# One reordered opening, one load queue and block-wise exponentials in a fused sparse-attention and three-way-maximum kernel

## The chip, the cores and the metric

The kernel runs on one core of a Trainium2 chip. The metric is device microseconds (us) of one execution, the median of several; lower is better. The core has a matrix engine (TensorE, PE in the profile, with its weight loads as PEld), a vector engine (VectorE, DVE), an activation engine (ScalarE, ACT), a general engine (GpSimd, POOL), a sequencer that only issues transfers here (SyncE, SP) and 16 DMA engines. Each engine works through its own instructions in order; semaphores tie them together.

## The reference

```python
# q, k, v: (8, 8, 576, 64); heads 0-3 local, heads 4-7 strided
scores = matmul(q, k.T) / sqrt(64)
mask_local   = (rel >= 0) & (rel < 32)                 # rel = row - column
mask_strided = (rel >= 0) & (column % 32 == row % 32)
attn = softmax(where(mask, scores, -1e9))              # max subtracted, sum + 1e-9
x = matmul(attn, v) -> (4608, 512)                     # heads beside one another
h = maximum(maximum(x @ w1, x @ w2), x @ w3)           # w1, w2, w3: (512, 768)
out = h @ w_out                                        # w_out: (768, 512)
```

The four weight matrices arrive as float32 bits that were widened on the host to 64-bit words; the kernel turns each of them into a high and a low part. The same is done with x and h, and every product is taken as three matmuls (high x high, high x low, low x high).

## The kernel before

**Units.** Attention is cut into 32 units, four for each of the 8 batches: two strided pairs of heads, then two local pairs (line 195). Unit n needs its queries and keys (`load_qk`, two transfers of 288 KB) and its values (`load_v`, four or five small transfers). Its steps are S (scores on PE into PSUM), X (on VectorE: the mask from batch 1 on, the row maximum and its subtraction), E (one exponential over the whole unit on ScalarE), N (on VectorE: sums, reciprocal, product, transpose), V (values on PE into the one PSUM tile `o`), H and L (the high part of x on ScalarE, the low part on VectorE).

**Chunks.** The feed-forward part runs over nine chunks of 512 rows. For a chunk, F0 to F17 are the 18 products with the blocks of w1, w2 and w3 (12 matmuls each), M the maxima behind them, O0 to O3 the products with w_out (18 matmuls each) and Q the stores. f0, f1 and g0, g1 are the halves of F0 and F1: f for the strided heads, g for the local ones.

**Weights.** 24 blocks of weights of 512 KB (w0 to w17 for F0 to F17, w18 to w23 for w_out) are converted on the chip, in five steps over four functions: A (line 145: magnitude of the high words, ScalarE; line 146: the low words, ScalarE; line 147: clamp, GpSimd), B (lines 158 and 161: bits put together, VectorE, with a quarter of the PSUM tile `o` as scratch), D (line 171: low bits added, GpSimd), C (line 179: high part, ScalarE; line 180: low part, GpSimd). The magnitude lives in one of three buffers of the pool `wk` from A to the end of C.

**The opening.** Chunk 0 is the opening: units 0 to 7, all 24 conversions, F0 to F17 and O0 to O3 of chunk 0, laid out by the string `OPENING` (lines 47 to 55), which is a fixed order of steps; each engine gets its instructions in that order and keeps it. From chunk 1 on a loop with fixed places does the rest (lines 513 to 552); the change doesn't touch it. Unit 8's scores (S8) are part of the opening, its later steps belong to chunk 1.

**Sharing in the opening.** V writes the four banks of `o`, H and L read them, and B uses columns of the last two of them: the waits in the trace show that V, H and B take turns. The scores of units 0 and 2 lie in a PSUM tile that is given up before f0, those of the others in a second one.

**Loads.** Two queues issue loads at the start (lines 479 to 493): SP takes the queries and keys of units 0 to 3 first, ScalarE's queue takes w0, the values of unit 0, w1 and w2. SP then takes v1, w3, v2, w4, v3, w5 to w8, q4, v4, w9 to w13, q5, v5 and the rest. Loads for units 6 on are issued behind S4, S5, V4 and so on.

Of the kernel before, what the change touches and what calls it, by code (L numbers as in the profile page):

```python
# [7 lines left out]
F32 = mybir.dt.float32  # L8
# [3 lines left out]
AF = mybir.ActivationFunctionType  # L12
ALU = mybir.AluOpType
AX = mybir.AxisListType

B, H, S, D = 8, 8, 576, 64
# [27 lines left out]

OPENING = """
S0 X0 S1 E0 N0 A0 X1 B0 D0 E1 V0 A1 S2 C0 A2 N1 B1 H0 B2 D1 L0 A3 S3 C1 A4 X2 E2 B3 B4 D2 D3 C2 D4 A5 X3
C3 C4 N2 V1 H1 A6 B5 D5 L1 f0 A7 E3 B6 B7 C5 V2 D6 A8 C6 N3 D7 H2 f1 B8 U4 S4 D8 C7 A9 L2 V3 C8 X4 H3 L3
A10 A11 B9 D9 B10 D10 g0 g1 E4 M0 F2 M1 C9 C10 F3 N4 A12 A13 M2 U5 B11 B12 M3 D11 B13 D12 D13 F4 S5 C11  # L50
M4 C12 A14 C13 F5 A15 M5 X5 B14 F6 M6 B15 E5 D14 F7 M7 A16 D15 C14 V4 F8 F9 C15 B16 M8 N5 A17 A18 B17
B18 D16 F10 M9 F11 M10 H4 D17 C16 S6 C17 D18 A19 A20 F12 M11 M12 X6 B19 B20 C18 F13 D19 E6 M13 A21 D20
F14 L4 C19 F15 N6 C20 A22 V5 M14 B21 H5 L5 B22 D21 A23 F16 B23 S7 D22 M15 C21 F17 C22 D23 V6 M16 M17 C23
O0 O1 Q0 X7 E7 H6 L6 Q1 N7 O2 V7 U8 O3 H7 Q2 Q3 L7 S8
"""


@with_exitstack
def fused_kernel(ctx, tc, qT, kT, qk_loc, qk_str, v_loc, v_str, m_loc, m_str, w1, w2, w3, w_out, out):
# [6 lines left out]
    att = ctx.enter_context(tc.tile_pool(name="att", bufs=2))  # L66
    hp = ctx.enter_context(tc.tile_pool(name="hp", bufs=NJ))
    hm = ctx.enter_context(tc.tile_pool(name="hm", bufs=2))
    wk = ctx.enter_context(tc.tile_pool(name="wk", bufs=3))

    xp = [ctx.enter_context(tc.tile_pool(name=f"xp{i}", bufs=1)) for i in range(2)]
    early = ExitStack()
# [65 lines left out]
    def convert_begin():  # L138


        raw, i, j = raws.pop(0)
        words = raw.rearrange("p (n two) -> p n two", two=2)
        low, high = words[:, :, 0], words[:, :, 1]
        mag = wk.tile([P, 512], F32, name="work")
        pin(nc.scalar.activation(out=mag, in_=high.bitcast(F32), func=AF.Abs))
        pin(nc.scalar.activation(out=low, in_=low.bitcast(U32), func=AF.Copy, scale=2.0**-29))
        pin(nc.gpsimd.tensor_scalar(out=mag, in0=mag, scalar1=W_MOST, scalar2=W_LEAST, op0=ALU.min, op1=ALU.max))  # L147
        begun.append((low, high, mag, i, j))

    converted = []  # L150

# [46 lines left out]
    def load_qk(n):  # L198
        if n >= len(units):
            return  # L200
        b, p = units[n]
        t = (io_early if n in (2, 3) else io).tile([P, 2, S], F32, name="qk_t", bufs=2)
        if b < EARLY:
            pin(nc.sync.dma_start(out=t[:, 0, :], in_=qT[b, p]))
            pin(nc.sync.dma_start(out=t[:, 1, :], in_=kT[b, p]))
        else:
            src = qk_loc[b - EARLY, p, 0] if p < 2 else qk_str[b - EARLY, p - 2].rearrange("p x s -> p (x s)")
            src = src.rearrange("p (x h s) -> p x h s", x=2, h=2)
            for h in range(2):
                hs = slice(h * D, (h + 1) * D)  # L210
                pin(nc.sync.dma_start(out=t[hs], in_=src[hs, :, h, :]))
        loaded[n] = [t.rearrange("p x s -> p (x s)")]
# [99 lines left out]
    def less_maximum(n):  # L312
        s_ps, s, wide, nm, at, axes, masked = state[n]
        if masked:
            flat, mask = masked
            pin(nc.vector.tensor_tensor(out=flat, in0=flat, in1=mask.broadcast_to(list(flat.shape)), op=ALU.add))
        mx = att.tile([P, 2, MS], F32, name="mx")
        pin(nc.vector.tensor_reduce(out=mx[:, :, :nm], in_=s, op=ALU.max, axis=axes))  # L318
        pin(nc.vector.tensor_tensor(out=s, in0=s, in1=wide(mx), op=ALU.subtract))  # L319

    def exponentials(n):
        s = state[n][1]
        pin(nc.scalar.activation(out=s, in_=s, func=AF.Exp, scale=SCALE))  # L323

    def probabilities(n):
        s_ps, s, wide, nm, at, axes, _ = state[n]
        sm = att.tile([P, 2, MS], F32, name="sm")

        sums = sm[:, :, :nm] if nm * at == 512 else s_ps[:, :, 512 - MS : 512 - MS + nm]
        pin(nc.vector.tensor_reduce(out=sums, in_=s, op=ALU.add, axis=axes))  # L330
        pin(nc.vector.tensor_scalar(out=sums, in0=sums, scalar1=EPS, scalar2=None, op0=ALU.add))
        pin(nc.vector.reciprocal(out=sm[:, :, :nm], in_=sums))
        pin(nc.vector.tensor_tensor(out=s, in0=s, in1=wide(sm), op=ALU.mult))  # L333
        state[n] = s_ps, nm, at
# [141 lines left out]
        pin(nc.scalar.dma_start(out=out[c * CH + t * P : c * CH + (t + 1) * P, :], in_=o_sb))  # L476


    for n in range(4):
        load_qk(n)  # L480
    pin(nc.scalar.activation(out=nothing, in_=nothing, func=AF.Exp))
    load_weights(1, nc.scalar)
    load_v(0, nc.scalar)
    load_weights(2, nc.scalar)
    load_v(1)
    for n in (2, 3):
        load_weights(1)
        load_v(n)
    for count, n in ((4, 4), (5, 5)):
        load_weights(count)  # L490
        load_qk(n)
        load_v(n)
    load_weights(len(sources))
    steps = {
        "U": paired_queries, "S": scores, "X": less_maximum, "E": exponentials, "N": lambda n: (probabilities(n), transposed(n)),
        "V": values, "H": leading, "L": rest,
        "A": lambda n: convert_begin(), "B": lambda n: convert_bits(), "D": lambda n: convert_add(),
        "C": lambda n: convert_end(),
        "F": lambda n: ff_in(0, n // 3, n % 3), "f": lambda n: ff_in(0, n // 3, n % 3, (2, 3)),
        "g": lambda n: ff_in(0, n // 3, n % 3, (0, 1)), "M": lambda n: ff_max(0, n // 3, n % 3),  # L500
# [118 lines left out]
```

## Time and profile before

| | |
|---|---|
| time, median of 3 runs | 707.14 us (707.0 to 708.51) |
| the profiled execution's own time | 705.32 us |
| its span, first to last instruction | 703.6 us |
| TensorE busy | 677.2 us (96%) |
| VectorE, ScalarE, GpSimd busy | 297.2, 188.8, 151.1 us |
| start of chunk 1 on TensorE (behind S8) | 122.99 us |
| moved by DMA | 55.67 MB |

The page cuts the span into 40 slices of 17.6 us, with one digit for each engine, and gives the granted clock of TensorE in tenths of full speed. Views by window give the busy time of each engine in a stretch; the timeline gives instructions with their start, duration and the idle time ahead of them; the waits sum that idle time by what ended it. GpSimd's last conversion, and TensorE's wait for it, stand near 107 us.

### The profile page before, as it was taken

To read this page: it belongs to the slowest core of one execution; us is meant where nothing else is said; L and a number is where in the kernel's file an instruction comes from. 1 tells how busy PE (TensorE), PEld (TensorE's weight loads), DVE (VectorE), ACT (ScalarE), POOL (GpSimd) and SP (SyncE) were. 2 spreads that over 40 slices of the span, in tenths; PEclk is the share of its full clock that TensorE was granted. 3 is DMA by queue.
4 is the path that set the end of the run, shared out by engine and by line. 5 is a ranking of instruction groups with operands and counts; after the bars stand their busy time and mean duration, and the time that the engine had idled before them with its cause. 6 is when DMAs were issued, how large, how long until landed. Compare 5 with 4: busy or idle time off the path is not lost.

```text
span 703.6 us, 16737 instructions
## 1 busy us (share of the span) xinstructions
PE 677.2 (96%) x7408; PEld 555.2 (79%) x7408; DVE 297.2 (42%) x507; ACT 188.8 (27%) x402; POOL 151.1 (21%) x153
## 2 busy tenths in 40 slices
PE   4579999999999999999999999999999999999997
PEld 3457877888888888878888888888888888888886
DVE  5788782754425540555145434544255101101110
ACT  2576653222122122222221312222212111111111
POOL 5789891011000110111011000110010101100120
PEclk9879999999999999999999999999999999999999
DMA  9998122312212221222211132223120010010001
GB/s 266 255 275 331 56 63 99 105 56 65 94 47 66 94 80 45 61 75 70 96 56 55 65 110 70 57 65 94 52 56 2 22 40 0 1 46 15 1 1 60
DMA packets 36081, 55.67 MB, mean 79 GB/s; under 512 B 5257, under 2 KB 18569, under 8 KB 36009
## 3 DMA queue, kind: packets, MB, share of 16 engines
q1 hardware_dynamic: 29060, 43.30, 21.1%
q10 hardware_dynamic: 6948, 11.31, 4.5%
q8 instruction: 58, 0.95, 0.6%
q14 instruction: 15, 0.11, 0.1%
HBM read 45.15 MB, written 9.44 MB: 78 GB/s over the span
## 4 chain that ended last, share of the span: by engine, by line
PE 84%; POOL 3%; DVE 1%; issue 1%; ACT 0%; DVEq 0%; ACTq 0%
PE f_ps L445 56%; PE f_ps L470 21%; PE o_ps L366 2%; PE o_ps L396 2%; PE s_ps L273 2%; PE s_ps L295 2%; POOL wNone L180 1%; POOL work L171 1%; POOL hl L461 0%; DVE work L161 0%; DVE o_ps L158 0%; POOL w L180 0%; POOL work L147 0%; DVE xl L428 0%; ACT xh L424 0%
## 5 line engine op out<-in xcount | busy, mean ns | idle before, releaser
L445 PE MATMUL f_ps<-xh,w 128*128 128x512 f32 x1296 | 410.2, 393 | 3.2 <-DVE pt L340 2.7
L445 PEld LDWEIGHTS f_ps<-xh,w 128*128 128x128 f32 x1296 | 244.3, 188 | 56.2 <-ACT w L179 2.7
L445 PE MATMUL f_ps<-xl,w 128*128 128x512 f32 x648 | 253.7, 391 | 0.9 <-DMA qk_t<-in_kT 0.5
L457 DVE TENSOR_TENSOR h_max<-f_ps,h_max 128x512 f32<-128x512 f32 x108 | 74.3, 688 | 290.6 <-PE f_ps L445 290.6
L461 POOL TENSOR_TENSOR hl<-h_max,hh 128x512 fp32r<-128x512 f32 x54 | 69.5, 1287 | 518.1 <-ACT hh L460 518.1
L445 PEld LDWEIGHTS f_ps<-xl,w 128*128 128x128 f32 x648 | 122.2, 189 | 26.5 <-DVE xl L428 1.9
L470 PE MATMUL f_ps<-wNone,hh 128*128 128x512 f32 x432 | 134.6, 392 | 0.5 <-POOL wNone L180 0.5
L470 PEld LDWEIGHTS f_ps<-wNone,hh 128*128 128x128 f32 x432 | 80.4, 188 | 17.8 <-POOL wNone L180 0.9
L460 ACT CAST hh<-h_max 128x512 fp32r<-128x512 f32 x54 | 33.4, 618 | 200.8 <-DVE h_max L457 200.8
L470 PE MATMUL f_ps<-wNone,hl 128*128 128x512 f32 x216 | 84.1, 389 | 0.0
L428 DVE TENSOR_TENSOR xl<-o_ps,xh 128x320 fp32r<-128x320 f32 (+11 forms) x96 | 28.3, 350 | 56.5 <-ACT xh L424 45.6
L475 ACT COPY work<-f_ps 128x512 f32<-128x512 f32 x36 | 21.2, 590 | 102.1 <-PE f_ps L470 102.1
L455 ACT COPY h_max<-f_ps 128x512 f32<-128x512 f32 x54 | 31.7, 588 | 60.4 <-POOL hl L461 33.1
L470 PEld LDWEIGHTS f_ps<-wNone,hl 128*128 128x128 f32 x216 | 40.6, 188 | 8.7 <-issue 0.2
L323 ACT ACTIVATE s_ps<-s_ps 128x640 f32<-128x640 f32 (+2 forms) x32 | 20.7, 648 | 91.7 <-DVE s_ps L319 84.1
L340 DVE STREAM_TRANSPOSE pt<-s_ps 128x640 f32<-128x640 f32 (+2 forms) x32 | 32.4, 1012 | 0.7
L424 ACT CAST xh<-o_ps 128x320 fp32r<-128x320 f32 (+11 forms) x96 | 24.3, 328 | 29.5 <-PE o_ps L396 18.8
L318 DVE TENSOR_REDUCE mx<-s_ps 128x10 f32<-128x640 f32 (+2 forms) x32 | 24.7, 772 | 6.7 <-PE s_ps L295 5.7
L333 DVE TENSOR_TENSOR s_ps<-s_ps,sm 128x640 f32<-128x640 f32 (+2 forms) x32 | 25.0, 780 | 1.1
L319 DVE TENSOR_TENSOR s_ps<-s_ps,mx 128x640 f32<-128x640 f32 (+2 forms) x32 | 25.0, 780 | 1.1
L295 PE MATMUL s_ps<-qk_t 64*32 64x64 f32 (+1 forms) x1408 | 19.7, 227 | 5.2 <-issue 3.1
L171 POOL TENSOR_TENSOR work<-work,w 128x512 int32<-128x512 int32 x18 | 23.2, 1299 | 5.2 <-DVE work L161 4.5
(52 smaller groups left out, 355.9 us busy)
## 6 DMA issues: line engine op xcount, KB each, us to landing
out<-work ACTq DMA_DIRECT2D x36, 256.0 KB, 2.1
qk_t<-in_qT SPq DMA_DIRECT2D x28, 288.0 KB, 3.9
qk_t<-in_kT SPq DMA_DIRECT2D x28, 288.0 KB, 4.8
w<-in_w SPq DMA_DIRECT2D x15, 512.0 KB, 8.2
v_t<-in_v_str SPq DMA_DIRECT2D x56, 128.0 KB, 3.3
v_t<-in_v_loc SPq DMA_DIRECT2D x48, 96.0 KB, 3.3
wNone<-in_w_out SPq DMA_DIRECT2D x6, 512.0 KB, 11.5
w<-in_w ACTq DMA_DIRECT2D x3, 512.0 KB
```

The costliest lines, as they stand in the source:

```text
L171: pin(nc.gpsimd.tensor_tensor(out=bits, in0=bits, in1=low, op=ALU.add))
L295: pin(nc.tensor.matmul(s_ps[32 * j : 32 * (j + 1), h, k1 : k1 + w], t[hs, q0 : q0 + 32], t[hs, k0 : k0 + w], start=not first, stop=not fir ...
L319: pin(nc.vector.tensor_tensor(out=s, in0=s, in1=wide(mx), op=ALU.subtract))
L333: pin(nc.vector.tensor_tensor(out=s, in0=s, in1=wide(sm), op=ALU.mult))
L340: pin(nc.vector.transpose(pt[:, :, : nm * at], s_ps[:, :, : nm * at]))
L428: pin(nc.vector.tensor_tensor(out=lo, in0=src, in1=hi.bitcast(F32), op=ALU.subtract))
L445: pin(nc.tensor.matmul(f_ps, w[:, kc, :], x[:, kc, :], start=(kc == 2 and n == 0), stop=(kc == 1 and n == 2)))
L455: pin(nc.scalar.copy(out=a, in_=f_ps))
L457: pin(nc.vector.tensor_tensor(out=a, in0=f_ps, in1=a, op=ALU.max))
L460: pin(nc.scalar.copy(out=hh, in_=a))
L461: pin(nc.gpsimd.tensor_tensor(out=hl, in0=a, in1=hh.bitcast(F32), op=ALU.subtract))
L470: pin(nc.tensor.matmul(f_ps, h[:, ts], w, start=(j == 0 and n == 0), stop=(j == NJ - 1 and n == 2)))
```

## The change

The string of the opening is replaced by another. The matmul groups of TensorE keep the same relative order up to F3 (S0, S1, V0, S2, S3, V1, f0, V2, f1, S4, V3, g0, g1, F2, F3); near the end V7 and S8 now stand ahead of O0, where they stood behind O2 and O3. The conversion's low-word step (line 146) becomes a step K of its own. The pool `wk` has four buffers instead of three. All loads are issued by SP, in the order `LOADS`. Three local units (3, 6 and 7) take a new step G in place of E: VectorE scales the row maximum by -0.125 and leaves the subtraction out, ScalarE does one exponential for each of 2 x 5 blocks of 64 columns with that maximum as bias and with the sum of the block as a second output, and N leaves its sums out.

```diff
--- before.py
+++ after.py
@@ -44,15 +44,19 @@
 
 
 
+
+LOADS = "q0 w0 w1 q1 v0 w2 q2 q3 w3 w4 v1 w5 w6 v2 w7 w8 v3 q4 v4 w9 w10 w11 w12 w13 q5 v5"
 OPENING = """
-S0 X0 S1 E0 N0 A0 X1 B0 D0 E1 V0 A1 S2 C0 A2 N1 B1 H0 B2 D1 L0 A3 S3 C1 A4 X2 E2 B3 B4 D2 D3 C2 D4 A5 X3
-C3 C4 N2 V1 H1 A6 B5 D5 L1 f0 A7 E3 B6 B7 C5 V2 D6 A8 C6 N3 D7 H2 f1 B8 U4 S4 D8 C7 A9 L2 V3 C8 X4 H3 L3
-A10 A11 B9 D9 B10 D10 g0 g1 E4 M0 F2 M1 C9 C10 F3 N4 A12 A13 M2 U5 B11 B12 M3 D11 B13 D12 D13 F4 S5 C11
-M4 C12 A14 C13 F5 A15 M5 X5 B14 F6 M6 B15 E5 D14 F7 M7 A16 D15 C14 V4 F8 F9 C15 B16 M8 N5 A17 A18 B17
-B18 D16 F10 M9 F11 M10 H4 D17 C16 S6 C17 D18 A19 A20 F12 M11 M12 X6 B19 B20 C18 F13 D19 E6 M13 A21 D20
-F14 L4 C19 F15 N6 C20 A22 V5 M14 B21 H5 L5 B22 D21 A23 F16 B23 S7 D22 M15 C21 F17 C22 D23 V6 M16 M17 C23
-O0 O1 Q0 X7 E7 H6 L6 Q1 N7 O2 V7 U8 O3 H7 Q2 Q3 L7 S8
+A0 S0 A1 X0 E0 K0 B0 N0 K1 S1 B1 A2 X1 V0 D0 E1 N1 D1 C0 H0 S2 C1 A3 B2 L0 X2 K2 D2 B3 K3 S3 E2 N2 A4 K4
+V1 D3 C2 A5 B4 X3 D4 C3 K5 H1 L1 B5 A6 C4 G3 D5 f0 B6 A7 K6 N3 V2 D6 A8 H2 L2 C5 K7 U4 B7 D7 B8 f1 A9 C6
+S4 K8 D8 C7 V3 H3 A10 C8 X4 K9 L3 K10 g0 g1 M0 B9 D9 F2 B10 A11 D10 M1 K11 E4 A12 C9 K12 U5 F3 N4 V4 C10
+A13 M2 K13 F4 A14 H4 B11 B12 B13 M3 D11 D12 S5 K14 B14 D13 D14 C11 M4 X5 C12 E5 F5 M5 F6 A15 A16 M6 F7
+N5 C13 L4 K15 F8 C14 M7 K16 A17 K17 B15 D15 S6 A18 F9 M8 X6 C15 F10 B16 G6 M9 D16 V5 B17 M10 D17 A19 B18
+H5 N6 F11 C16 F12 S7 K18 D18 C17 A20 K19 M11 B19 C18 U8 L5 F13 B20 D19 A21 V6 X7 K20 M12 A22 K21 M13 C19
+B21 D20 B22 F14 G7 D21 K22 F15 A23 D22 M14 H6 F16 M15 N7 K23 C20 M16 B23 C21 L6 F17 S8 V7 C22 D23 M17
+C23 O0 H7 Q0 O1 O2 Q1 Q2 O3 L7 Q3
 """
+APART = [int(step[1:]) for step in OPENING.split() if step[0] == "G"]
 
 
 @with_exitstack
@@ -66,7 +70,7 @@
     att = ctx.enter_context(tc.tile_pool(name="att", bufs=2))
     hp = ctx.enter_context(tc.tile_pool(name="hp", bufs=NJ))
     hm = ctx.enter_context(tc.tile_pool(name="hm", bufs=2))
-    wk = ctx.enter_context(tc.tile_pool(name="wk", bufs=3))
+    wk = ctx.enter_context(tc.tile_pool(name="wk", bufs=4))
 
     xp = [ctx.enter_context(tc.tile_pool(name=f"xp{i}", bufs=1)) for i in range(2)]
     early = ExitStack()
@@ -143,9 +147,15 @@
         low, high = words[:, :, 0], words[:, :, 1]
         mag = wk.tile([P, 512], F32, name="work")
         pin(nc.scalar.activation(out=mag, in_=high.bitcast(F32), func=AF.Abs))
+        pin(nc.gpsimd.tensor_scalar(out=mag, in0=mag, scalar1=W_MOST, scalar2=W_LEAST, op0=ALU.min, op1=ALU.max))
+        lows.append(low)
+        begun.append((low, high, mag, i, j))
+
+    lows = []
+
+    def convert_low():
+        low = lows.pop(0)
         pin(nc.scalar.activation(out=low, in_=low.bitcast(U32), func=AF.Copy, scale=2.0**-29))
-        pin(nc.gpsimd.tensor_scalar(out=mag, in0=mag, scalar1=W_MOST, scalar2=W_LEAST, op0=ALU.min, op1=ALU.max))
-        begun.append((low, high, mag, i, j))
 
     converted = []
 
@@ -316,18 +326,37 @@
             pin(nc.vector.tensor_tensor(out=flat, in0=flat, in1=mask.broadcast_to(list(flat.shape)), op=ALU.add))
         mx = att.tile([P, 2, MS], F32, name="mx")
         pin(nc.vector.tensor_reduce(out=mx[:, :, :nm], in_=s, op=ALU.max, axis=axes))
+        if n in APART:
+            state[n] += (mx,)
+            pin(nc.vector.tensor_scalar(out=mx[:, :, :nm], in0=mx[:, :, :nm], scalar1=-SCALE, scalar2=None, op0=ALU.mult))
+            return
         pin(nc.vector.tensor_tensor(out=s, in0=s, in1=wide(mx), op=ALU.subtract))
+
+    def exponentials_apart(n):
+
+        s_ps, s, wide, nm, at, axes, _, mx = state[n]
+        sm = att.tile([P, 2, MS], F32, name="sm")
+        for h in range(2):
+            for m in range(nm):
+                pin(nc.scalar.activation(
+                    out=s[:, h, m], in_=s[:, h, m], func=AF.Exp, scale=SCALE, bias=mx[:, h, m : m + 1],
+                    accum_out=sm[:, h, m : m + 1],
+                ))
+        state[n] = s_ps, s, wide, nm, at, axes, sm
 
     def exponentials(n):
         s = state[n][1]
         pin(nc.scalar.activation(out=s, in_=s, func=AF.Exp, scale=SCALE))
 
     def probabilities(n):
-        s_ps, s, wide, nm, at, axes, _ = state[n]
-        sm = att.tile([P, 2, MS], F32, name="sm")
-
-        sums = sm[:, :, :nm] if nm * at == 512 else s_ps[:, :, 512 - MS : 512 - MS + nm]
-        pin(nc.vector.tensor_reduce(out=sums, in_=s, op=ALU.add, axis=axes))
+        s_ps, s, wide, nm, at, axes, sm = state[n]
+        if n in APART:
+            sums = sm[:, :, :nm]
+        else:
+            sm = att.tile([P, 2, MS], F32, name="sm")
+
+            sums = sm[:, :, :nm] if nm * at == 512 else s_ps[:, :, 512 - MS : 512 - MS + nm]
+            pin(nc.vector.tensor_reduce(out=sums, in_=s, op=ALU.add, axis=axes))
         pin(nc.vector.tensor_scalar(out=sums, in0=sums, scalar1=EPS, scalar2=None, op0=ALU.add))
         pin(nc.vector.reciprocal(out=sm[:, :, :nm], in_=sums))
         pin(nc.vector.tensor_tensor(out=s, in0=s, in1=wide(sm), op=ALU.mult))
@@ -476,25 +505,15 @@
         pin(nc.scalar.dma_start(out=out[c * CH + t * P : c * CH + (t + 1) * P, :], in_=o_sb))
 
 
-    for n in range(4):
-        load_qk(n)
     pin(nc.scalar.activation(out=nothing, in_=nothing, func=AF.Exp))
-    load_weights(1, nc.scalar)
-    load_v(0, nc.scalar)
-    load_weights(2, nc.scalar)
-    load_v(1)
-    for n in (2, 3):
-        load_weights(1)
-        load_v(n)
-    for count, n in ((4, 4), (5, 5)):
-        load_weights(count)
-        load_qk(n)
-        load_v(n)
+    loads = {"q": load_qk, "v": load_v, "w": lambda n: load_weights(1)}
+    for step in LOADS.split():
+        loads[step[0]](int(step[1:]))
     load_weights(len(sources))
     steps = {
-        "U": paired_queries, "S": scores, "X": less_maximum, "E": exponentials, "N": lambda n: (probabilities(n), transposed(n)),
+        "U": paired_queries, "S": scores, "X": less_maximum, "E": exponentials, "G": exponentials_apart, "N": lambda n: (probabilities(n), transposed(n)),
         "V": values, "H": leading, "L": rest,
-        "A": lambda n: convert_begin(), "B": lambda n: convert_bits(), "D": lambda n: convert_add(),
+        "A": lambda n: convert_begin(), "K": lambda n: convert_low(), "B": lambda n: convert_bits(), "D": lambda n: convert_add(),
         "C": lambda n: convert_end(),
         "F": lambda n: ff_in(0, n // 3, n % 3), "f": lambda n: ff_in(0, n // 3, n % 3, (2, 3)),
         "g": lambda n: ff_in(0, n // 3, n % 3, (0, 1)), "M": lambda n: ff_max(0, n // 3, n % 3),
```

## Rows read from the trace of the kernel before

**Rows 1.** The page's second part: granted clock of TensorE in 40 slices
```profile
PEclk9879999999999999999999999999999999999999
```

**Rows 2.** Windows: busy of each engine, granted clock, DMA share, GB/s
```profile
122.99:703.60 580.61, 576.23 (x5655) 475.62 (x5648) 212.73 (x362) 122.34 (x270) 61.71 (x48) 1.00 0.18 55
...
47.12:122.99 75.87, 73.84 (x851) 58.72 (x844) 52.15 (x88) 42.55 (x86) 54.90 (x51) 1.00 0.45 142
...
0.00:47.12 47.12, 27.16 (x916) 20.84 (x916) 32.33 (x58) 23.92 (x46) 34.50 (x55) 0.82 0.95 273
...
9.91:48.94 39.03, 23.43 (x704) 17.13 (x699) 31.30 (x57) 23.68 (x48) 28.82 (x29) 0.78 0.98 272
...
46.23:107.65 61.42, 59.33 (x698) 47.05 (x698) 48.29 (x76) 36.70 (x69) 55.78 (x53) 1.00 0.51 159
```

**Rows 3.** Waits of TensorE, 0 to 125 us: total, times, longest
```profile
PE o_ps L407 <- DVE work L161: 7.1, 2, 4.7
```

**Rows 4.** Timeline of TensorE: start, duration, [idle ahead, ended by]
```profile
28.85 1.99 PE L407 MATMUL o_ps<-pt,v_t 18*64 18x18 f32 x128 [4.69 <-DVE work L161]
...
48.87 0.50 PE L445 MATMUL f_ps<-xl,w 128*128 128x512 f32 x1 [0.41 <-DVE xl L428]
...
107.69 0.50 PE L470 MATMUL f_ps<-wNone,hh 128*128 128x512 f32 x1 [0.47 <-POOL wNone L180]
...
121.92 1.14 PE L273 MATMUL s_ps<-qk_t,pt 64*64 64x36 f32 x64
```

**Rows 5.** Timeline of VectorE
```profile
9.91 0.47 DVE L330 TENSOR_REDUCE s_ps<-s_ps 128x16 f32<-128x288 f32 x1 [1.20 <-ACT s_ps L323]
...
27.32 0.69 DVE L158 TENSOR_SCALAR o_ps<-work 128x512 int32<-128x512 int32 x1 [2.16 <-POOL work L147]
...
30.30 0.82 DVE L330 TENSOR_REDUCE s_ps<-s_ps 128x10 f32<-128x640 f32 x1
...
32.49 0.85 DVE L340 STREAM_TRANSPOSE pt<-s_ps 128x640 f32<-128x640 f32 x1
...
48.06 0.88 DVE L428 TENSOR_TENSOR xl<-o_ps,xh 128x480 fp32r<-128x480 f32 x3
```

**Rows 6.** Timeline of ScalarE
```profile
25.93 0.66 ACT L145 ACTIVATE work<-w 128x512 f32<-128x512 f32 x1 [2.41 <-DMA w<-in_w]
```

**Rows 7.** VectorE's groups by shape, 0 to 110 us: count | busy, mean ns
```profile
L158 DVE TENSOR_SCALAR o_ps<-work 128x512 int32<-128x512 int32 x24 | 16.6, 691 | 7.6 <-POOL work L147 3.4 <-ACT xh L424 1.5 <-POOL wNone L180 0.8
...
L161 DVE SCALAR_TENSOR_TENSOR work<-w,o_ps 128x512 int32<-128x512 int32 x18 | 12.4, 687 | 1.0
...
L319 DVE TENSOR_TENSOR s_ps<-s_ps,mx 128x640 f32<-128x640 f32 x4 | 3.3, 832 | 0.1
```

**Rows 8.** GpSimd's groups, 9 to 110 us
```profile
L147 POOL TENSOR_SCALAR work<-work 128x512 f32<-128x512 f32 x24 | 14.8, 618 | 6.8 <-ACT work L145 4.9 <-DMA v_t<-in_v_loc 1.8
```

**Rows 9.** Timeline of GpSimd
```profile
7.78 0.89 POOL L111 COPY mpair<-mstr 32x18 f32<-32x18 f32 x4
...
15.72 1.29 POOL L171 TENSOR_TENSOR work<-work,w 128x512 int32<-128x512 int32 x1 [4.49 <-DVE work L161]
...
44.95 1.28 POOL L180 TENSOR_TENSOR w<-work,w 128x512 fp32r<-128x512 f32 x1
...
106.36 1.29 POOL L180 TENSOR_TENSOR wNone<-work,wNone 128x512 fp32r<-128x512 f32 x1
```

**Rows 10.** ScalarE's groups by shape, whole span
```profile
L323 ACT ACTIVATE s_ps<-s_ps 128x288 f32<-128x288 f32 x2 | 0.8, 395 | 10.5 <-DMA v_t<-in_v_str 7.2 <-DVE s_ps L319 3.3
...
L424 ACT CAST xh<-o_ps 128x64 fp32r<-128x64 f32 x12 | 2.6, 218 | 3.6 <-PE o_ps L396 3.2 <-PE o_ps L366 0.4
...
L481 ACT ACTIVATE nothing<-nothing 128x1 f32<-128x1 f32 x1 | 0.2, 203 | 0.0
```

**Rows 11.** Windows of the load phase, same columns as group 2
```profile
15.00:20.00 5.00, 4.46 (x132) 3.20 (x132) 3.87 (x8) 3.77 (x7) 4.12 (x5) 1.00 0.94 205
...
30.00:35.00 5.00, 2.35 (x66) 1.89 (x58) 4.21 (x8) 3.69 (x8) 4.99 (x5) 0.50 1.07 364
```

## The prediction, made before the change was run

> **What bounds the kernel now.** The page's row of granted clocks comes first: the reader is to see that only the second to fourth slice is below full speed [rows 1]. Windows then cut the span where TensorE's stream changes. Up to 47.12 us TensorE is busy for 27.16 us at a mean clock of 0.82; from 47.12 to 122.99 it is busy 73.84 of 75.87 us, and from there, where chunk 1 starts, 576.23 of 580.61 us [rows 2]. The change touches only the opening, so I keep the last 580.61 us as they are and ask when chunk 1 starts. I call that time T; it is 122.99.
>
> The waits say what the early idle time is. TensorE's largest one is V0 and V1 waiting 7.1 us for VectorE's bit step [rows 3], 4.69 us of it in one piece ahead of V1 at 28.85, and the clock falls inside that slice of the page [rows 1, 4]. The timeline has two more places that count. At 48.87 TensorE waits for L3, the last vector step of unit 3, which ends at 48.94; after it the stream is nearly closed. At 107.69 it waits 0.47 for GpSimd's last weight part [rows 4], the end of conversion C23 at 107.65. So two chains must both move for T to move: VectorE up to L3, and GpSimd up to C23. TensorE itself has slack of 20 us in the first 47.
>
> **VectorE up to L3.** From N0 (9.91) to the end of L3 (48.94) VectorE is busy 31.30 of 39.03 us [rows 2, 5]. It runs 57 instructions with gaps of about 0.04 between neighbours (the 0.69 of line 158 to the next start), some 2.2 us, so about 5.5 us are real waiting. One piece of it is 2.16 at 27.32, for the clamp of the fifth weight [rows 5]; behind it stands ScalarE's A4 at 25.93, which waited 2.41 for w4's load [rows 6].
>
> Now the new order, walked through queue by queue with these durations. GpSimd builds masks until 8.67 [rows 9], so clamp 0 ends near 9.3 and B0 starts at 9.35, now ahead of N0. N0 ends at 13.0, B1 at 14.4, X1 at 15.4. E1 costs 0.5 of waiting, then N1 to 18.1, B2, L0 to 20.3, X2 to 22.2, B3, N2 to 26.6 (a full N takes 3.04, from 30.30 to 33.34 [rows 5]), B4, X3 at 29.0, L1, B5, B6 to 32.6. In this order w4 is the eighth load and not the tenth, and A4 waits for E2 (22.9) and no longer for a load.
>
> *Saved work.* Unit 3 drops the subtraction (0.83 [rows 7]) and the sum (0.82 [rows 5]) and adds a scaling of ten columns (about 0.2: the 1.37 between that sum and the transpose hold the product, 0.83, and two such small steps with their gaps [rows 5]): 1.45 less. Units 6 and 7 save as much each, where VectorE is not what TensorE waits for; I count that at nothing, hidden by TensorE's own stream, and if the cover is gone it is a gain of at most 2.9.
>
> *The new wait.* G3 is ten exponentials of 64 columns with a sum each. No row shows an exponential with a sum output. The nearest row by size is the cast of 64 columns, 0.218; ten are 2.2, the low end. The high end is ten times the 288-column exponential and a shortest ScalarE instruction for the sum, 0.395 + 0.203, so 6.0 [rows 10]. I take the 64-column row with one shortest instruction for reading the sum, 0.42, so 4.2 in place of one exponential. G3 can start near 29.9, behind C4, and ends at 34.1; N3 waits for it 1.55. Behind G3 on ScalarE stand A7, K6, A8, H2 and C5, and GpSimd's D6 waits for K6 (35.2): that is in the walk.
>
> The Trainium skill ("ScalarE: Activation LUTs", What ACT_TABLE_LOAD costs, and its rules for kernel authors) speaks against small blocks: a fixed part near 0.3 us for each activation with a per-partition bias, whatever its length, and 0.83 ns an element. By it G3 would be about 3.5, an estimate from that page, and by my rows 4.2; N3 would then start 0.7 earlier. No run so far shows such a block.
>
> N3 ends at 36.3, L2 at 37.5, B7 and B8 at 40.35, X4 at 42.7, L3 at 43.6. As a check: 31.30 - 1.45 busy, 2.1 of gaps, 2.5 of waits (0.5 E1, 0.2 S2, 1.55 G3, 0.3 H2) on 9.35 make 43.75. I take 43.7, so L3 is 5.2 earlier. Low end: no waiting, 41.2. High end: all of the old 5.5 us of waits, 46.8. V3 and S4 are ready by then (S4 at 40.2 behind the query copies, V3 behind B8 at 41.6).
>
> **Loads.** A single queue costs nothing if transfers come in time. Adding up the sizes in the new order, w2 ends after 3.05 MB, w4 after 5.28, v3 after 8.39, q4 after 8.98. From 30 to 35 us SP alone moved 364 GB/s, from 15 to 20, while it issued small value transfers, 205 [rows 11]. I take 280, the middle: from 1.8 us on and 0.7 to land w2 comes at 13.4, w4 at 21.4, v3 at 32.5 and q4 at 34.6. The walk wants them at 11.4, 22.9, 40 and 37.2; w2's delay of 2 us vanishes behind E1, because C0 waits for E1 on ScalarE until 15.9 anyway. ScalarE loses its load issues, which I count at nothing (E0 is not on the path once B0 goes first).
>
> **GpSimd up to C23.** D0 waited 4.49 for B0 and started at 15.72 [rows 9]; now it starts near 13. The same walk has clamps 0 to 9, adds 0 to 8 and C7 done at 44.7. Before, C7 ended at 46.23 [rows 9] with one clamp fewer (0.62 [rows 8]), so GpSimd is 2.1 ahead. From there to C23 it was busy 55.78 of 61.42 us [rows 2]. The fourth buffer lets clamps go earlier, but adds still wait for VectorE and casts for ScalarE with its two further G; I leave the 5.6 us of waiting as they are. C23 then ends at 107.65 - 2.1 = 105.5; the low end, without waiting, is 99.9.
>
> **The sum.** TensorE's side: T = 122.99 - 5.2 = 117.8. G6 adds about 0.8: it stands on ScalarE ahead of M9, which frees a product's PSUM buffer, ends 4.0 us after F9 and delays M9 to 4.6, while F10 and V5 cover only 2.7 + 1.07 (a chunk takes 580.61 / 8 = 72.6; less eight attention groups of 1.07 that leaves 0.222 for each of 288 products, twelve for F10). So 118.6. GpSimd's side: before, T came 15.34 behind C23; V7 and S8 (1.07 each from start to start, S8 at 121.92 [rows 4]) now stand ahead of O0, so 13.2 remain: 105.5 + 13.2 = 118.7. Both sides meet; T = 118.7, 4.3 us earlier. The span is 118.7 + 580.6 = 699.3, with the 1.72 around it (705.32 - 703.6) 701.0. The profiled execution was 1.82 below the median of 707.14, so I forecast 702.8.
>
> **Rivals.** First, conversions that don't come sooner: C23 stays at 107.65, since every stage keeps waiting for the next. For it: GpSimd was busy for 91% of that stretch. Against it: a head start of 2.1. T = 107.65 + 13.2 = 120.85, 705.0.
>
> Second, the clock. The mean of 0.82 over 47.12 us [rows 2] is 17 us at the lower of the two levels, and they follow the pause of 4.69 ahead of V1 [rows 4]. The new pause behind f1 (35.2 to 39.1) is nearly as long; the old one goes, since V1 comes at 23.6, right behind S3. If the clock falls at 39, S4 delays X4 by 1.07 and the twelve products of g0 and g1 lose about as much again behind L3, 2.3 in all: 705.1.
>
> Third, better: G near its low end and few waits give L3 at 42.1 and C23 at 102.8 at the latest; T = 116.0, 700.1.
>
> Fourth, slower: the single queue stays at the rate that it shows among small transfers, 205 GB/s, since v1, v2 and v3 lie between the weights that feed the walk. Then q4 lands at 46.3; the query copies (1.35), S4 (1.07), X4 (2.3) and L3 follow one another to 52.0, 3.1 behind the old L3: 710.2. It decides from the point at which q4 lands later than about 43, that is below some 221 GB/s. Against it: big transfers keep the engines busy while small ones are issued, share 0.94 even at 205 [rows 11].
>
> That the change doesn't do what it says would show in G: at 6.0 each, N3 loses 1.8 and M9 1.8 more, 706.4.
>
> **Chances.** Forecast 0.47 (701 to 704.5), better 0.14, conversions 0.13, clock 0.13, dear G 0.04, slow queue 0.09. A measurement here can tell 0.2%, 1.4 us: faster means below 705.7. The forecast and the better case lie there, and most of conversions and clock (0.19 of 0.26): 0.80. Same gets the rest of these and the dear G, about 0.10, slower the slow queue and a little for what I have not thought of, 0.10. The range goes from 698.5 (L3 at its low end, 699.4, and TensorE's two waits of 0.41 and 0.47 gone [rows 4]) to 707.5, past the dear G, and leaves out the slow queue.
>
> **What would show it.** L3's end (43.7), C7 (44.7), C23 (105.5), the duration of a G (4.2), chunk 1's start (118.7), and the clock in the second to fourth slice of the page. The prediction fails if loads make ScalarE wait at A2 to A9 for more than 3 us in all, if TensorE waits for C23 by more than 1 us, or if chunk 1 starts later than 121.6.

## The result, and the profile after

The changed kernel takes 711.0 us (median of 20 runs, 707.63 to 714.03), the kernel before 707.48 beside it (20 runs, 704.12 to 709.43): a ratio of 1.0047, 95% interval 1.0032 to 1.0061. The forecast was 702.8 and faster; the kernel is 0.47% slower. The profiled execution took 707.63, the shortest of the 20, that of before 705.32; so the two traces lie 2.3 us apart and the medians 3.5. The traces below show where time goes, the runs how much; a usual execution of the changed kernel is 3.4 us longer than the one traced.

The page first: span, busy times, granted clock.

```profile
span 705.9 us, 16785 instructions
...
PE 678.7 (96%) x7408; PEld 555.6 (79%) x7408; DVE 295.5 (42%) x504; ACT 197.6 (28%) x459; POOL 151.1 (21%) x153
...
PEclk9779999999999999999999999999999999999999
```

VectorE lost 1.7 us of work and ScalarE gained 8.8; the clock's dip is that of [rows 1], a tenth deeper in one slice. TensorE's waits up to 130 us (total, times, longest) answer to [rows 3]:

```profile
PE s_ps L305 <- DMA qk_t<-in_kT: 5.7, 2, 5.4
PE o_ps L436 <- issue: 5.0, 2, 2.7
...
PE o_ps L395 <- DVE work L171: 2.5, 2, 2.0
PE f_ps L474 <- ACT h_max L484: 2.1, 2, 1.8
PE f_ps L474 <- DVE h_max L486: 1.6, 1, 1.6
...
PE o_ps L436 <- DVE work L171: 0.2, 1, 0.2
```

V0 and V1 waited 7.1 us for VectorE's bit step before; that is now 0.2, as the new order meant it. In its place stands "issue", 5.0, a wait for nothing that the profile shows. TensorE's timeline says where, and answers to [rows 4]:

```profile
14.36 1.47 PE L436 MATMUL o_ps<-pt,v_t 18*64 18x18 f32 x85 [0.17 <-DVE work L171]
18.53 0.88 PE L436 MATMUL o_ps<-pt,v_t 18*64 18x18 f32 x43 [2.71 <-issue]
...
26.24 0.80 PE L436 MATMUL o_ps<-pt,v_t 18*64 18x18 f32 x60
...
29.36 1.26 PE L436 MATMUL o_ps<-pt,v_t 18*64 18x18 f32 x68 [2.32 <-issue]
...
65.59 0.50 PE L474 MATMUL f_ps<-xh,w 128*128 128x512 f32 x1 [1.64 <-DVE h_max L486]
...
83.71 0.50 PE L474 MATMUL f_ps<-xh,w 128*128 128x512 f32 x1 [1.83 <-ACT h_max L484]
...
124.89 0.39 PE L474 MATMUL f_ps<-xh,w 128*128 128x512 f32 x1
```

V0 (128 products of 18 columns) stops after 85 of them, V1 after 60, in the middle of runs of equal products, with no releaser named. In the transfers of 15.5 to 18.6 us there is one packet of a queue of its own (packets, MB, share), and again one in those of 26.5 to 29.4:

```profile
q1 hardware_dynamic: 973, 1.10, 103.6%
q8 instruction: 1, 0.02, 1.9%
```

TensorE waits for its own instructions, beside loads that take the 16 DMA engines' whole time in the first of these windows and 87.8% of it in the second. The profile doesn't say so in words; three readings do. Windows of 0.2 us place the two packets at 16.1 and 26.7, and V0 goes on at 18.53, V1 at 29.36, 2.4 and 2.7 us later; in the kernel before a packet at 10.1 is followed by S1 going on at 12.52. The queue has 58 packets in the whole execution, and 56 in the kernels below that have 256 pairs of weight load and product, 512 instructions, fewer. And four more matmuls put ahead of V0 move its stop by four (the early mask below). The Trainium skill ("Runtime: NRT & Kernel Launch", Instruction fetch mechanics) says that an engine's code comes in blocks of 16 KiB, 256 instructions, by a queue of its own, and that crossing a block is mostly hidden. The block agrees: two packets for 512 instructions, 0.02 MB each, and the stop in V0 lies 127 pairs (42 of S1, 85 of V0) behind the place at which S1 stopped before. That it is hidden doesn't: 2.71 and 2.32 us here.

VectorE then (answering to [rows 5]): L3 ends at 47.16 + 0.89 = 48.05, against 48.94 before and 43.7 forecast.

```profile
20.25 0.69 DVE L168 TENSOR_SCALAR o_ps<-work 128x512 int32<-128x512 int32 x1 [2.26 <-ACT xh L453]
...
30.74 0.69 DVE L168 TENSOR_SCALAR o_ps<-work 128x512 int32<-128x512 int32 x1 [1.59 <-PE o_ps L436]
...
32.92 0.69 DVE L331 TENSOR_SCALAR mx<-mx 128x10 f32<-128x10 f32 x1
...
38.51 0.17 DVE L360 TENSOR_SCALAR sm<-sm 128x10 f32<-128x10 f32 x1 [1.14 <-ACT s_ps L341]
...
47.16 0.89 DVE L457 TENSOR_TENSOR xl<-o_ps,xh 128x480 fp32r<-128x480 f32 x3
```

Bit step B4 now waits for V1: the wait has changed sides. On GpSimd, C7 and C23 (ends 49.11 and 112.00, forecast 44.7 and 105.5; [rows 9]), and the windows that answer to [rows 2]:

```profile
47.81 1.30 POOL L190 TENSOR_TENSOR w<-work,w 128x512 fp32r<-128x512 f32 x1
...
110.69 1.31 POOL L190 TENSOR_TENSOR wNone<-work,wNone 128x512 fp32r<-128x512 f32 x1
```

```profile
48.05:124.89 76.84, 73.08 (x842) 58.18 (x841) 51.58 (x84) 47.50 (x121) 56.22 (x52) 1.00 0.47 146
30.62:48.05 17.43, 12.74 (x248) 8.69 (x249) 15.11 (x27) 14.26 (x45) 13.88 (x14) 0.60 0.93 277
```

Chunk 1 starts at 124.89: L3 is 0.89 earlier, but it is 76.84 from there where it was 74.05. The 2.8 more are made by the waits of 1.64 for M4 (VectorE, behind B14) and 1.83 for M9 (ScalarE, behind G6), where all waits of TensorE behind L3 came to 1.6 before, and by the clock: the first five of the twelve products of g0 and g1 run at the lower level, 0.43 us from one to the next for 0.23, about 1 us.

### The profile page after: what moved, and what is told of

It is laid out like the page before. It is cut to its first block, busy times and chain, and to the rows that moved or that the text cites. A ratio compares the mean times of both kernels' runs of the same rounds, so it can differ in the third digit from the quotient of the medians.

```text
span 705.9 us, 16785 instructions
## 1 busy us (share of the span) xinstructions
PE 678.7 (96%) x7408; PEld 555.6 (79%) x7408; DVE 295.5 (42%) x504; ACT 197.6 (28%) x459; POOL 151.1 (21%) x153
## 4 chain that ended last, share of the span: by engine, by line
PE 86%; DVE 4%; POOL 3%; ACT 3%; issue 3%; POOLq 0%; DVEq 0%; ACTq 0%
PE f_ps L474 57%; PE f_ps L499 21%; PE o_ps L395 2%; PE o_ps L425 2%; PE s_ps L305 2%; PE s_ps L283 2%; ACT s_ps L341 2%; DVE o_ps L168 1%; DVE work L171 1%; POOL work L181 1%; POOL w L190 1%; POOL work L150 1%; POOL mloc L97 0%; PE o_ps L436 0%; DVE xl L457 0%
## 5 line engine op out<-in xcount | busy, mean ns | idle before, releaser
L349 ACT ACTIVATE s_ps<-s_ps 128x576 f32<-128x576 f32 (+2 forms) x29 | 18.6, 643 | 85.1 <-DVE s_ps L333 81.1
L305 PEld LDWEIGHTS s_ps<-qk_t 64*32 64x32 f32 x1408 | 16.2, 113 | 9.6 <-issue 7.5
```

The lines of the kernel that those rows point to most:

```text
L305: pin(nc.tensor.matmul(s_ps[32 * j : 32 * (j + 1), h, k1 : k1 + w], t[hs, q0 : q0 + 32], t[hs, k0 : k0 + w], start=not first, stop=not fir ...
```

## Experiments

Kernels named "a" start from the changed kernel, "b" from the kernel before. Ratios are to the kernel before on the same chip.

**The parts by themselves.** One queue, with its new order of loads, on the old order of work:

```diff
+LOADS = "q0 w0 w1 q1 v0 w2 q2 q3 w3 w4 v1 w5 w6 v2 w7 w8 v3 q4 v4 w9 ..."
-    load_weights(1, nc.scalar)
-    load_v(0, nc.scalar)
...
+    for step in LOADS.split():
+        loads[step[0]](int(step[1:]))
```

> The kernel before with only the loads changed: one queue, the new order. Stalls theory (the changed kernel loses on TensorE's stops inside V0 and V1 and on block-wise exponentials that stand ahead of other ScalarE work; the loads are nearly neutral): 0 to 2 us below the kernel before, because w4 comes sooner and the 2.16 us wait of VectorE for the fifth clamp shrinks. Loads theory (the single queue brings q1 and w2 too late): 2 to 4 us above it.

Measured: 706.59 against 707.42, 0.9977 (0.9962 to 0.9993). A small gain. The same edit undone on the new order:

> The changed kernel with the loads of before (two queues, old order). Stalls theory: within 1.5 us of the changed kernel, some 709 to 712, since the stops in V0 and V1 and the waits behind G6 stay. Loads theory: 706 to 708, with A2 starting before 12 us and D0 before 12.5.

Measured: 708.73, 1.0020 (1.0009 to 1.0030), less than the 1.0047 of the changed kernel. So the queue with its order of loads helps the one order of work and not the other.

Exponentials by unit again, in the new order (G3, G6, G7 become E3, E6, E7):

> The changed kernel with one exponential for each of units 3, 6 and 7 (E in place of G; the subtraction and the sum are back on VectorE). Stalls theory: TensorE's wait for M9 (1.83 us) goes and VectorE's wait for G3 (1.14) goes, VectorE has 1.5 more work in front of L3: 1.5 to 3 us below the changed kernel. Loads theory: within 1 us of the changed kernel.

Measured: 707.59, 1.0003 (0.9989 to 1.0017). The block exponentials make up all that the change lost, 3.3 us; order and queue together give nothing. The reverse, G3, G6 and G7 for the E's of the old order:

> The kernel before with block-wise exponentials for units 3, 6 and 7 at the places where its whole ones stood. Stalls theory: 4.4 us on ScalarE in place of 0.7 delays what is queued behind (A, C and M steps): 1 to 3 us above the kernel before. Loads theory: no change within 1 us.

Measured: 711.29, 1.0052 (1.0036 to 1.0069), 3.9 us lost. Its largest wait of TensorE that the kernel before lacks is for a copy on ScalarE, ahead of a unit's scores:

```profile
PE s_ps L282 <- ACT pt L259: 2.5, 1, 2.5
```

**Which of the G's.** M9 ahead of G6 on ScalarE:

```diff
-... F10 B16 G6 M9 D16 V5 ...
+... F10 B16 M9 G6 D16 V5 ...
```

> The changed kernel with M9 ahead of G6 in the order. Order theory (G6 costs by standing ahead of M9): TensorE's wait of 1.83 us for M9 goes and the time falls by 1 to 2 us, unless C23 (112.0) then holds O0. Rival (what counts is ScalarE's longer work as a whole, by way of C23): C23 and the time stay within 0.7 us.

Measured: 708.92, 1.0026 (1.0004 to 1.0048). TensorE's wait for M9 is gone from its trace, and one of 1.27 ahead of V6, for VectorE's bit step, stands there instead. E3 for G3 alone:

> The changed kernel with a whole exponential for unit 3 alone (E3 in place of G3). If the cost of the blocks sits in front of L3: 2 to 3.5 us below the changed kernel, near the kernel with three whole exponentials. If it sits behind L3, at G6 and G7: within 1 us of the changed kernel.

Measured: 708.67, 1.0022 (1.0002 to 1.0043). They give back 0.0021 and 0.0025 of the 1.0047, 1.5 and 1.8 us; the intervals overlap that of the changed kernel, so these two are likely rather than shown, and only the sum of the three G's is firm.

**TensorE's code.** 64 small products more (128 pairs), overwritten later, ahead of S1:

```diff
+        if n == 1:
+            ...
+            for m in range(MS):
+                for j in range(4):
+                    for h in range(2):
+                        ...
+                        pin(nc.tensor.matmul(s_ps[...], t0[...], t0[...], start=True, stop=True))
```

> The changed kernel with 64 more small products (128 more TensorE instruction pairs, those of S0 once more into the place of S1, which its mask then overwrites) at the point where TensorE idles 5.4 us for q1. Code theory (TensorE's stops inside V0 and V1 are instruction fetches, one per some 128 pairs, which take 4 to 5 us each beside the loads, so the pace of S0 to V1 is set by the amount of code): V1 ends 2 to 5 us later than at 30.6, L3 likewise, and the time is 1 to 4 us above the changed kernel. Rival (the stops come from transfers or semaphores of the work itself): the products vanish in the idle time, V1's end and the time stay within 1 us.

Measured (4 runs): 713.7, 1.0089 (1.0070 to 1.0107), 3.0 us beyond the changed kernel for products that run about 1.5. V1 ends at 35.90 instead of 30.62, and V0 stops after the same 85 products, for longer:

```profile
18.44 0.66 PE L316 MATMUL s_ps<-qk_t 64*32 64x18 f32 x42 [2.22 <-issue]
...
26.57 0.88 PE L447 MATMUL o_ps<-pt,v_t 18*64 18x18 f32 x43 [6.06 <-issue]
```

256 pairs fewer: the scores and values of units 0 and 1 as one bfloat16 pass (of lower precision) instead of the two of float32:

```diff
... (the same for the scores)
-                        v[js, h, m, :],
-                        pt[js, h, m * 32 : m * 32 + NI],
+                        as_read(n, v[js, h, m, :]),
+                        as_read(n, pt[js, h, m * 32 : m * 32 + NI]),
```

> The changed kernel with the products of S0, S1, V0 and V1 taken on the upper halves of the float32 words (bfloat16), one pass in place of two, which lowers the precision of units 0 and 1: 256 TensorE instruction pairs fewer in the first 31 us. Code theory: no stop over 1 us inside V0 and V1, V1 ends before 28, L3 before 46, 1.5 to 4 us below the changed kernel. Rival: VectorE's chain stays where it is, V1's end moves by under 1 us and the time by under 1 us.

Measured: 708.96, 1.0023 (1.0009 to 1.0037). V1 ends at 26.24, behind a stop of 3.51 that now stands at the end of S3, and L3 at 43.98 + 0.89 = 44.87, near the forecast 43.7; but chunk 1 starts at 122.68, 77.81 behind it. TensorE waits for M4 and M9 on the way, and the granted clock is low until 47.5 and again from 81.6 to 85.0:

```profile
25.17 0.42 PE L306 MATMUL s_ps<-qk_t 64*32 64x64 f32 x2 [3.51 <-issue]
...
62.62 0.50 PE L475 MATMUL f_ps<-xh,w 128*128 128x512 f32 x1 [1.03 <-DVE h_max L487]
...
80.71 0.50 PE L475 MATMUL f_ps<-xh,w 128*128 128x512 f32 x1 [1.80 <-ACT h_max L485]
```

C23 ended at 109.00, and TensorE did not wait for it: O0 to O3 run without a break from 106.22. The same edit on the kernel before:

> The kernel before with the products of S0, S1, V0 and V1 in one pass on the upper halves of the words, which lowers the precision of units 0 and 1: 256 instruction pairs fewer. Forecast from the prediction's walk (before, V0 and V1 wait for VectorE's bit steps, and the code arrives inside those waits): V1 moves by under 1 us and the time by under 1 us, so code supply binds in the new order alone. Rival (code supply binds both): V1 ends 2 us or more sooner than at 30.8 and the time falls by 1.5 us or more.

Measured: 708.52, 1.0009 (0.9996 to 1.0023): no gain. V1 ended at 30.99 (30.84 before), since it waits for another thing there:

```profile
30.28 0.71 PE L408 MATMUL o_ps<-pt,v_t 18*64 18x18 bf16 x64 [7.60 <-DMA w<-in_w]
```

**Does it matter where the stop falls?** S2's two mask products, which need nothing, go ahead of V0:

```diff
-... A2 X1 V0 D0 ...
+... A2 X1 P2 V0 D0 ...
```

> The changed kernel with one step moved on TensorE: the two mask products of S2 (2.5 us of work in 4 instruction pairs) ahead of V0 instead of behind it. Code theory: the same code in the same amount, but the next block of instructions arrives while the long products run, so TensorE's stop inside V0 falls from 2.7 to under 1.2 us, S2 ends some 2 us earlier than at 23.1, V1 ends before 29.5; 1 to 2.5 us below the changed kernel. Rival (the stop is tied to V0's own operands): the stop stays over 2 us and V0 ends 2.5 us later; time not below the changed kernel.

Measured: 710.59, 1.0047 (1.0032 to 1.0062), no gain. The stop in V0 comes after 81 products instead of 85, four earlier for the four matmuls put ahead of it (each mask product takes two), and shrinks; a new one in S3 takes its place, that in V1 stays, and V1 ends at 30.05:

```profile
18.20 0.69 PE L442 MATMUL o_ps<-pt,v_t 18*64 18x18 f32 x47 [0.70 <-issue]
...
24.40 0.90 PE L311 MATMUL s_ps<-qk_t 64*32 64x64 f32 x68 [1.64 <-issue]
...
28.79 1.26 PE L442 MATMUL o_ps<-pt,v_t 18*64 18x18 f32 x69 [1.97 <-issue]
```

The three stops sum to 4.31 us where the two of the changed kernel had 5.03: the shift changed mostly which product meets the edge of a block. On the old order with one queue:

> The kernel before with the one load queue and with S2's mask products ahead of V0. Code theory: 0.5 to 2.5 us below the kernel with the one queue alone (706.6), as V0 waits 2.4 us for its bit step there anyway. Rival: no change within 0.7 us.

Measured: 706.7 against 706.61, 0.9996 (0.9982 to 1.0010).

**Loads for S1 first** (q1 ahead of w0 and w1), since S1 waited 5.41 for its keys:

```diff
-LOADS = "q0 w0 w1 q1 v0 w2 ..."
+LOADS = "q0 q1 w0 w1 v0 w2 ..."
```

> The changed kernel with q1 loaded ahead of w0 and w1. Code theory: S1 starts near 7.5 to 9 in place of 12.7, so its blocks of code are taken sooner; the stops inside V0 and V1 shrink by 2 us or more in all, V1 ends before 29, 1 to 2.5 us below the changed kernel. Rival (w0 and w1, now later, start the conversions later): B0 starts after 10.5, V1's end stays, time within 1 us of the changed kernel or above it.

Measured: 710.8, 1.0062 (1.0048 to 1.0075). The wait for keys goes, S1 and V1 stop for code instead, and V1 ends at 33.23:

```profile
11.68 0.66 PE L305 MATMUL s_ps<-qk_t 64*32 64x18 f32 x42 [3.46 <-issue]
...
31.97 1.26 PE L436 MATMUL o_ps<-pt,v_t 18*64 18x18 f32 x68 [5.23 <-issue]
```

On the old order with one queue, and on the mended order below:

> The kernel before with the one load queue, q1 ahead of w0 and w1. Code theory: 0.5 to 2 us below the kernel with the one queue in the new order (706.6). Rival: no change within 0.7 us.

Measured: 706.58 against 706.82, 0.9998 (0.9983 to 1.0014).

> The mended kernel (whole exponentials, S2's mask products ahead of V0, H4 earlier, the last two low parts on VectorE) with q1 ahead of w0 and w1. Code theory: 1 to 2.5 us below the mended kernel (707.4), so that it beats the kernel before by 1 us or more. Rival: no change within 1 us.

Measured: 710.36, 1.0053 (1.0040 to 1.0067). The idea fell in all three.

**The new order mended.** E for the three G's, the early mask, H4 ahead of K13 and A14 on ScalarE (so that B14 and M4 come sooner), and the low parts of the last two weights on VectorE (the last two are shown):

```diff
-... A13 M2 K13 F4 A14 H4 B11 ...
+... A13 M2 H4 K13 F4 A14 B11 ...
-        pin(nc.gpsimd.tensor_tensor(out=lo, in0=mag, in1=hi.bitcast(F32), op=ALU.subtract))
+        last = nc.vector if i is None and j >= NJ - 2 else nc.gpsimd
+        pin(last.tensor_tensor(out=lo, in0=mag, in1=hi.bitcast(F32), op=ALU.subtract))
```

> The changed kernel with whole exponentials for units 3, 6 and 7, S2's mask products ahead of V0, H4 ahead of K13 and A14 (so that M4 isn't late behind B14), and the low parts of the last two weights on VectorE in place of GpSimd. Stalls theory: TensorE's wait for M4 (1.6) falls under 0.6, C23 ends before 108.5, chunk 1 starts before 121.5 and the time is 2 to 5 us below the kernel before. Rival (GpSimd's chain holds O0 whatever is mended in front): within 1.5 us of the kernel with whole exponentials (707.6).

Measured: 707.37 against 706.61, 1.0004 (0.9986 to 1.0022). The wait ahead of F6 fell from 1.64 to 0.54; but L3 ended at 48.30, and chunk 1 started at 123.90, 75.6 behind it. C23, its low part now on VectorE, ended at 110.87, no sooner than in the kernel with the three E's (110.77): taking this work off GpSimd did not bring it forward. The time came out as the rival had it, but not for its reason, since TensorE did not wait for C23.

```profile
109.50 1.37 DVE L191 TENSOR_TENSOR wNone<-work,wNone 128x512 fp32r<-128x512 f32 x1 [1.22 <-ACT wNone L189]
```

The mended order with the 256 pairs fewer (same lower precision in units 0 and 1):

> The mended order with units 0 and 1 in one bfloat16 pass (256 pairs of weight load and product fewer, lower precision in these two units). Two-chains theory: with less code L3 ends near 45 (44.87 with less code alone), and with the last two low parts on VectorE C23 ends near 106, so neither side holds the other: chunk 1 starts at 45 + 75.6 = 120.6, 3 us ahead of either mend alone, and the ratio to before is 0.995 to 0.998. Rival, that each stage only passes its lateness on: chunk 1 starts at 122.5 to 124 as in each mend alone, and the ratio stays at 1.000 to 1.003.

Measured: 704.92 against 707.22, 0.9972 (0.9959 to 0.9985). V1 comes without a stop for code, L3 ends at 44.19, and chunk 1 starts at 118.72, where the forecast had 118.7. C23 ends at 105.70, 5.2 earlier than with the mended order alone, though nothing of its own work changed:

```profile
23.70 0.66 PE L444 MATMUL o_ps<-pt,v_t 18*64 18x18 bf16 x64 [2.08 <-DVE work L171]
...
118.72 0.39 PE L482 MATMUL f_ps<-xh,w 128*128 128x512 f32 x1
```

The stretch behind chunk 1's start, which the change doesn't touch, took 583.08 us in this trace and 580.61 in that of the kernel before. So the 4.3 us won at chunk 1 left 1.8 in the span (701.8 for 703.6) and 2.3 in the medians; what took the rest is open, though TensorE's waits without a releaser come to 1.5 there and to 0.6 before.

**The clock.** Five more copies of f0's first product and three of f1's, overwritten, fill the pause in which the granted clock stays at its lower level:

```diff
+        if heads == (2, 3):
+            for _ in range(5 if i == 0 else 3):
+                pin(nc.tensor.matmul(f_ps, wh[:, 2, :], hi[:, 2, :], start=True, stop=True))
```

> The mended kernel with the first product of f0 done five times more and that of f1 three times more (overwritten, so only work is added, where TensorE idles). Clock theory: the clock is back at 2.4 GHz before 45 us in place of 51.6, the products behind L3 run at full speed and the time falls by 0.7 to 2 us. Rival (the low clock only fills idle time): no gain, or up to 1 us more for the added products.

Measured: 706.21 against 706.82, 0.9993 (0.9977 to 1.0009), not to be told from the mended order's 1.0004. On the old order with one queue:

> The kernel before with the one load queue and with the first product of f0 five times and that of f1 three times more (overwritten, work alone). If the clock returns before 47 and counts: 0.5 to 2 us below the kernel with the one queue (706.6), 1.5 to 3 us below the kernel before. Rival: it is the same as the kernel with the one queue within 0.7 us.

Measured: 704.58 against 707.61, 0.9956 (0.9939 to 0.9974), which beats both kernels with the computation as it was. Its rows of f0 and f1: 0.63 us for a product at the lower level, 0.39 at the higher. The clock is back at 40.9 and stays; in the same kernel without the extra products it was back at 47.2, fell again at 50.6 and was back at 54.0.

```profile
38.64 0.63 PE L449 MATMUL f_ps<-xl,w 128*128 128x512 f32 x1
...
43.14 0.97 PE L446 MATMUL f_ps<-xh,w 128*128 128x512 f32 x3
...
44.18 0.39 PE L449 MATMUL f_ps<-xl,w 128*128 128x512 f32 x1
```

## Why the prediction was wrong

**What bounds the kernel: right of L3, not shown of GpSimd.** The same 256 pairs taken out of the mended order brought L3 4.1 us forward (48.30 to 44.19) and chunk 1 5.2 (123.90 to 118.72). That GpSimd up to C23 is a second chain beside it is not shown for the new order. C23 came 5.2 earlier between the same two kernels, so there it follows the others, and TensorE hardly waits for it: from the start of O0 to chunk 1 it takes 16.73 us in the changed kernel and 16.45 in those with less code, with the mended order and with both, a wait of 0.28 at most. In the old order it did wait, 0.47, as the prediction read. Which end holds chunk 1 once L3 is early is therefore open; what stands between L3 and chunk 1 in the less-code kernel are the waits for M4 and M9 and the clock.

**The step that failed: the walk to L3.** It has V0 behind B1 (14.4) and V1 at 23.6, right behind S3, with products end to end: none of its waits up to L3 (0.5 E1, 0.2 S2, 1.55 G3, 0.3 H2) is for TensorE's code. V0 began on time (14.36) but ended at 19.41, V1 ended at 30.62, so the old 30.84 hardly moved. TensorE's timeline of before has such a stop, in a row that I had not used:

```profile
12.52 0.66 PE L295 MATMUL s_ps<-qk_t 64*32 64x18 f32 x42 [2.54 <-issue]
```

In the old order V0 and V1 waited for VectorE anyway (2.36 and 4.69), and a packet of code came within each of these waits, at 14.4 and at 24.8; taking away those waits uncovered the stops for code. That code holds up the new order and not the kernel before is shown by the 256 pairs taken out: V1 ends 6.5 us sooner in the mended order (30.85 to 24.36) and the time falls from 1.0004 to 0.9972, their intervals apart; in the kernel before, V1 and the time stay. How much of it belongs to the single queue is open. With it the old order has the stops too, 2.26 in V0 behind the same wait of 2.37 for VectorE, and 3.56 in V1; with two queues the new order has none in V0 and V1, but V0 waits 6.35 for its bit step there. From V0 and V1 VectorE got the waits that the walk lacked: 2.26 ahead of B2, 0.78 for S2, 1.59 ahead of B4. L3 came 4.35 late. (The check of the walk adds up to 43.8, not 43.75; that changes nothing.)

**G: its length right, its price too low.** Ten pairs of rows like these, 0.43 to 0.44 from one block to the next, make a G of 4.34 (78.83 to 83.17; forecast 4.2, high end 6.0):

```profile
82.55 0.19 ACT L341 ACTIVATION_READ_ACCUMULATOR s_ps<-s_ps,mx 128x1 f32 x1
82.77 0.29 ACT L341 ACTIVATE s_ps<-s_ps,mx 128x64 f32<-128x64 f32 x1
...
83.08 0.58 ACT L484 COPY h_max<-f_ps 128x512 f32<-128x512 f32 x1
```

I had charged 1.55 at N3 against 1.45 saved, and 0.8 at M9: about 0.9 in all. N3's wait was 1.14, M9's 1.83, and the runs put the three G's at 3.3 us (new order) and 3.9 (old). Not priced were what else queues on ScalarE, as the copies ahead of S4 (2.5 in the old order) and casts that GpSimd needs (C23 came 1.2 later with G than without), and the scaling, which took 0.69 and not 0.2. How the 3.3 us divide among these is open: the traces with and without G lie only 1.1 apart at the start of chunk 1 (124.89 and 123.81).

**GpSimd.** D0 was to start near 13, but in the new order it stands on GpSimd behind the clamp of w2, whose load the same walk has at 13.4; it started at 16.09. With less code, where V0 doesn't stop, B2 began behind it at 18.76, 0.7 after the walk's 18.1. C7 was to end at 44.7; it ended at 49.11, behind the late bit steps, so the head start of 2.1 became a delay of 2.9. The 5.6 us of later waits that I kept became 62.89 - 55.15 = 7.7 between 49.11 and 112.00. The 13.2 from C23 to chunk 1 were 12.89, with a wait of TensorE for C23 of 0.3, so this lateness cost little by itself.

**Loads.** w2 was to land at 13.4; A2 began at 14.76 after 3.22 of waiting, past the 3 us that I gave as a sign of failure. The fourth rival, a slow queue, did not come about: the copies of unit 4's queries (41.76) waited for no load. What one queue is worth by itself I had put at nothing; with its order of loads it gained 0.23% on the old order of work. Why the new order is better off with two (1.0020 against 1.0047) no run settles: V1 ends at 29.77 there, 0.9 sooner, without a stop for code. And the two variants of the old order with one queue and another small edit read 0.9996 and 0.9998, so that the 0.23% may itself be partly luck.

**The clock**, the second rival, came true in part: it did not fall at 39 but, nearly as before (28.6), at 28.2; it was back at 41.8, fell again at 45.2, after the waits ahead of S4 and V3 (0.95 and 0.52), and was back at 48.6 instead of 45.6. That is about 1 us of the loss.

**The last stretch.** I kept the 580.61 us behind chunk 1's start as they were. That held in the changed kernel (581.01), not in the one kernel that started chunk 1 on the forecast (583.08).

**The side.** Of the slower outcomes I had named only the slow queue. The mechanism that happened, a wait that takes the place of the one removed, was asked of L3 and of G, not of TensorE's own supply.

## What to carry to other kernels

A row of "issue" in the middle of a run of equal instructions was here TensorE's own code coming late; before a wait elsewhere on that engine is taken away, add up how much code must come in by then. Small work on an engine off the path is priced by all that queues behind it, not by its one named reader. Before two late ends are called two chains, see whether one of them moves when only the other is mended.

## What the runs showed that I had not expected

- TensorE's code stops are of very different length in the same code: V1 behind 2.32 us in the changed kernel, 5.50 in the kernel with E3, whose order is the same up to there (row below). Part of the spread of 6.4 us over its 20 runs may come from this; no run shows how much.

```profile
32.43 1.26 PE L436 MATMUL o_ps<-pt,v_t 18*64 18x18 f32 x68 [5.50 <-issue]
```

- A VectorE scaling of ten columns took 0.69 us at 32.92 (the row above), while a like one at 38.51 took 0.17. GpSimd's add ran from 32.29 to 33.58, and the slow scaling ended at 33.61; the scalings of units 6 and 7 (1.03 and 0.68) end 0.04 and 0.03 us behind a GpSimd instruction as well. The Trainium skill ("SBUF — State Buffer", SBUF: two separate sides, on the port pair that VectorE and GpSimd share) says that, for some kinds of VectorE instruction, whichever starts first holds the pair for its whole instruction and the other waits; the ends agree.

```profile
32.29 1.29 POOL L181 TENSOR_TENSOR work<-work,w 128x512 int32<-128x512 int32 x1 [2.28 <-issue]
```

- Reading a sum out is an instruction of its own on ScalarE, 193 ns beside the 288 ns of its 64-column exponential: two fifths of a G.
- Overwritten products in a pause brought the clock back at 40.9 for good (47.2, with a second fall until 54.0, without them), and the time with them was 0.9956 against 0.9977 without; the two intervals overlap, so the gain is likely and not shown.
